# Scales of later weights found through DRAM, and spreads of keys and queries paced

## The chip, the cores and the metric

The kernel runs on one core of a Trainium2 chip. Its engines work side by side, each through its own queue of instructions in order: TensorE (PE; PEld is its loading of weights), VectorE (DVE), ScalarE (ACT), GpSimd (POOL) and SyncE (SP), whose queue issues nearly all transfers here. The metric is the device time of one execution in microseconds, and the median of several runs.

## The reference

Two attention layers of 32 heads with 20 features each read the same `x` (2048 rows of 640), and a gate per row mixes their outputs:

```python
def _A_ref(x, wqkv, wo):                      # _B_ref does the same with its own weights
    qkv = (x @ wqkv).reshape(B, S, 3, H, Dh).transpose(2, 0, 3, 1, 4)
    q, k, v = qkv[0], qkv[1], qkv[2]
    p = softmax(einsum("bhqd,bhkd->bhqk", q, k) * Dh ** -0.5, axis=-1)
    o = einsum("bhqk,bhkd->bhqd", p, v)
    return o.transpose(0, 2, 1, 3).reshape(B, S, D) @ wo

g = sigmoid((x * gate_w).sum(-1, keepdims=True))
return g * _A_ref(A_x, A_wqkv, A_wo) + (1 - g) * _B_ref(A_x, B_wqkv, B_wo)
```

All inputs and the output are float32.

## The kernel before, in words

**Numbers.** A product of float32 numbers is made from float16 parts: every operand is multiplied by a power of two, so that its largest number lies well in float16's range, and split into a high and a low part. So each kind of weight needs its largest absolute value over all 128 partitions. `largest` (L233) finds it in each partition on VectorE; a generator, `scales` (L167), carries it over the partitions: TensorE transposes the 128 maxima into one row (L173), VectorE takes the row's maximum (L177), four operations on bits make the power and its inverse (`powers`, L159), two products with the identity put them on a diagonal (L183), TensorE multiplies this by ones, which gives every partition both numbers (L190), and VectorE copies them out (L193) and hands them on (`set_qk`, `set_v`, or the function in `scales_o`). The first call, at the start, is for `x` and the first weights (five maxima). Twelve more stand among the work: three for queries and keys (two maxima each), seven for values and two for the output weights (one each).

**Staging.** Both layers together are 16 groups of four heads. A group takes 32 steps: four blocks of 512 queries, and for each eight steps over pairs of 128 keys. In a step TensorE makes eight products of scores (L639), ScalarE takes their exponentials (L642), and TensorE weighs the values of the step before (L657, in two blocks `V`). Beside this, 15 steps ahead, TensorE makes the scores again in the other direction (L581) and VectorE finds each query's maximum (L592, L589). The remaining room, one or two blocks of a step, goes to projections and output products (L382). Scores land in seven banks that rotate; who empties a bank (ScalarE or VectorE) frees it.

**What sets the order.** The program writes its own order: the strings `STEP` list a step's scores (`e`), maxima (`m`), blocks of values (`V`) and slots for one block of other work (`X`). Work with a date hangs in `todo` (`at(step, f)`); blocks wait in `fill` with a first step and a due step. Generators in `side` are moved on by `advance()`, once for each score, so eight times a step: such a move is called a turn, and a `yield` in a generator waits for the next. A generator that yields `PRODUCT` is parked until the next block of values, and its small product is put right ahead of that.

**Spreads.** A group's projected keys and queries lie in `cq` (two halves of 1024 tokens, `hl`), and `spread` (L433) copies them into the rows of `KT` and `QT` that the products want: 18 transfers a half, through `rows` (L424; issued in L428 and L430), all on SP's queue, one a turn. `spread_differences` (L474) adds four from `dd` to `KD`. The generator `later` (L490) starts them, a half at a time, ten turns after the half is projected and not before the group ahead has begun. When both halves are ready by then, both generators run side by side, and a turn has two transfers. `next_maxima` asks `spread_done` before a group's maxima are made.

**Other users of SP's queue** are the queries' maxima, which go through DRAM (`m_scr`: stored in L613, loaded in L617, five turns apart), the attention's outputs (L763), and the output products: `out_tiles` (L692) loads a tile of attention outputs (`o_in`, L699) and the sum so far (`y_out`, L704), waits `OWAIT` turns, and then puts its products in `fill`; their store is L732. SP executes its queue in order, a transfer that has to wait holds those behind it.

The body of the loop that calls all this:

```python
for what in (STEP[blocks] if maxima or some else LATE + " X" * (blocks == 2)).split():
    ...
    if what[0] == "e":
        ...
        advance()
    elif what == "V":
        product()
        if G:
            values(G - 1, k - 1)
```

Of the kernel before, what the change touches and what calls it, by code (L numbers as in the profile page):

```python
# [3 lines left out]

# [7 lines left out]
F32 = mybir.dt.float32  # L12
I32 = mybir.dt.int32
AF = mybir.ActivationFunctionType
OP = mybir.AluOpType
AX = mybir.AxisListType
# [3 lines left out]
P = 128  # L20
# [18 lines left out]
QUARTERS = (0, 128, 256, 384, 512)  # L39
FINE = (2, 3, 5, 6)  # L40
OB = 3
OWAIT = 20
AFROM, ADUE, ADUES = -24, -8, 4
QKMAX = (0, 10, 42, 10)
VEARLY = 338
# [23 lines left out]
def kernel(  # L69
# [48 lines left out]
    o_scr = [dram.tile([2, D, S], F16, name=f"o_scr{z}") for z in range(2)]  # L118
    m_scr = [dram.tile([4, 16, P], F16, name=f"m_scr{i}") for i in range(2)]
    y_scr = dram.tile([NT, P, D], F32, name="y_scr")  # L120


    clock = {"pe": 0.0, "done": 0.0, "act": 0.0, "dve": 0.0}
# [43 lines left out]
    def scales(maxima, n, then):  # L167

        for _ in range(REST):
            yield  # L170
        yield PRODUCT
        i, pt = take()
        nc.tensor.transpose(pt[:n, :P], maxima[:, :n], ident)  # L173
        tick_block(0.1, free_at[i])
        yield
        e = wts.tile([5, 8], F32, name="e", tag="scl", bufs=2)
        nc.vector.tensor_reduce(e[:n, 0:1], pt[:n, :P], axis=AX.X, op=OP.max)  # L177
        give(i, spend("dve", 0.3, clock["done"]))
        spend("dve", 1.0)
        powers(e.bitcast(I32)[:n, :], 1)  # L180
        dg = wts.tile([5, 2, 5], F32, name="dg", tag="scd", bufs=2)
        for k in range(2):
            nc.vector.tensor_scalar(dg[:n, k, :n], ident[:n, :n], e[:n, 3 + k:4 + k], None, op0=OP.mult)  # L183
        for _ in range(REST):
            yield
        yield PRODUCT
        i, pb = take()
        tick_block(0.1, free_at[i])
        for k in range(2):
            nc.tensor.matmul(pb[:, k * n:(k + 1) * n], ones[:n, :], dg[:n, k, :n], start=True, stop=True)  # L190
        yield
        both = wts.tile([P, 10], F32, name="both", tag="scb", bufs=2)
        nc.vector.tensor_copy(both[:, :2 * n], pb[:, :2 * n])  # L193
        give(i, spend("dve", 0.2, clock["done"]))
        then(both[:, :n], both[:, n:2 * n])

    def set_x(r_x, r, inv):
        nc.vector.tensor_copy(r_x, r)
        nc.vector.tensor_copy(inv_x, inv)

    def set_qk(i, r, inv):
        nc.vector.tensor_copy(r_qk[i], r)
        e = esc[i]
        nc.vector.tensor_tensor(e, inv[:, 0:1], inv_x, op=OP.mult)
        nc.vector.tensor_scalar(e, e, inv[:, 1:2], float(DH ** -0.5 / QKS ** 2), op0=OP.mult, op1=OP.mult)
        nc.vector.tensor_tensor(e, e, inv_x, op=OP.mult)

    def set_v(gg, r, inv):
        nc.vector.tensor_copy(r_v[gg], r)

        f = gg % (NG // 2) * 160
        while f < (gg % (NG // 2) + 1) * 160:
            p0 = f % P
            n = min(P - p0, (gg % (NG // 2) + 1) * 160 - f, (P, 32, 64, 32)[p0 // 32])
            nc.vector.tensor_copy(wrow[gg // (NG // 2)][p0:p0 + n, f // P:f // P + 1], inv[p0:p0 + n])
            f += n

    def scales_qk(i, maxima):

        return scales(maxima, 2, lambda r, inv: set_qk(i, r, inv))  # L220

    def scales_v(gg, maxima):
        return scales(maxima, 1, lambda r, inv: set_v(gg, r, inv))

    def scales_o(z, maxima):
        def then(r, inv):
            nc.vector.tensor_copy(r_o[z], r)
            nc.vector.tensor_scalar(f_o[z], gates[:, z, :], inv, inv_x, op0=OP.mult, op1=OP.mult)
            nc.vector.tensor_scalar(f_o[z], f_o[z], 1.0 / QKS, None, op0=OP.mult)

        return scales(maxima, 1, then)

    def largest(dst, src):  # L233
        nc.vector.tensor_reduce(dst, src, axis=AX.XY, op=OP.max,
# [198 lines left out]
    def spread(g, hl, t0, n, q=(0, 1), k=(0, 1), queues=repeat(nc.sync)):  # L433
# [5 lines left out]
        for j in range(2):  # L439
# [7 lines left out]
            if 1 in q:  # L447
# [2 lines left out]
                f = slice(r0 + 12 * j, r0 + 12 + 20 * j)  # L450
                yield from rows(qt[:, 1, cols], base, 8 * (1 - j), rk[g // 4][f, :, cols], 12 + 8 * j, False, queues)

    def project_r(i, ch):
        n = slice(ch * QB, (ch + 1) * QB)
        yield from project_chunk(blk["r", i], rk[i][:, 0, n], rk[i][:, 1, n], ch, QUARTERS if 4 * i in FINE else THIRDS)
        r_done.add((i, ch))
# [24 lines left out]
    def project_a(g, ch):  # L481
        if ch % 2 == 0:
            half_tiles(g)
        hl = blk["q", g]
        n = slice((ch % 2) * QB, (ch % 2 + 1) * QB)
        yield from project_chunk(blk["a", g], hl[:, 0, n], hl[:, 1, n], ch, QUARTERS if g in FINE else THIRDS)
        if ch == 1:
            key_differences(g, hl, work.tile([P, QB], F32, name="fs"), work.tile([P, 2, QB], F16, name="dd", bufs=1))
        if ch % 2 == 1:
            def later():  # L490
                for _ in range(10):
                    yield
                while not {(g // 4, c) for c in (ch - 1, ch)} <= r_done or now[0] < (g - 1) * NQ * NS + 1:
                    yield
                if ch == 1:
                    yield from spread_differences(g)
                yield from spread(g, hl, ch // 2 * 1024, 1024)
                spread_done.add((g, ch // 2))

            side.append(later())  # L500
# [478 lines left out]
    def at(G, f):  # L979
        todo.setdefault(G, []).append(f)  # L980
# [11 lines left out]
    for g in range(2 * NG):  # L992
        b = g * step
        n = g + 1
        if n < 2 * NG:
            parts = 4 if n in FINE else 3
            fill += [((-8, 15)[g] if g < 2 else b + AFROM, b + ADUE + ADUES * ch if g else 4 + 3 * ch, parts, project_a(n, ch))
                     for ch in range(4)]
            if n + 1 < 2 * NG:
                tasks(b + 2 if g else 9, 3, weights_a(n + 1))  # L1000
            i = g // 4 + 1
            if i < 4:
                if g % 4 == 0:
                    z, c0 = i // 2, 320 * (i % 2)
                    srcs = max_tasks([[(wqkv[z], part * D + c0 + 160 * k) for k in range(2)] for part in range(2)],
                                     lambda m, i=i: scales_qk(i, m))
                    tasks(b + QKMAX[i], 2, srcs)
                if g % 4 == 2:
                    tasks(b + 6, 3, weights_r(i))
                    parts = 4 if 4 * i in FINE else 3  # L1010
                    fill += [(b + 12, b + 22 + 4 * ch, parts, project_r(i, ch)) for ch in range(4)]
            gg = g // 2 + 1
            if gg < NG and g % 2 == 0:
                load, scale, split = weights_v(gg)
                at(max(b - 8, 0), load)
                if gg < NG - 1:
                    at(max(b - 5, 3), lambda scale=scale: side.append(scale()))
                at(max(b - 1, 7), split)
                fill += [(max(b + 2, 10), b + 2 * step - 4 + j // 2, 2, project_v(gg, j)) for j in range(0, NT, 2)]
    early = weights_v(NG - 1)  # L1020
    at(VEARLY, early[0])
# [164 lines left out]
```

## Time and profile before

| | |
|---|---|
| median of 3 runs | 2802.12 us (2801.08 to 2802.19) |
| the profiled execution | 2800.33 us, span 2798.5 us |
| mean granted TensorE clock | 0.995 |
| TensorE, VectorE, ScalarE, GpSimd busy | 98%, 88%, 90%, 24% |
| score products L639 | 4096, 1051.7 us |
| weighing of values L657 | 8192, 1082.2 us |
| issue of one spread on SP (kt<-cq, L428), median | 797 ns |
| DMA, mean busy share of 16 engines | 16.9% by the hardware queue q1 |

A row of waits reads "engine tile line <- who released it: us in total, times, longest us". A row of the timeline has the start in us from the span's start, the time in us, engine, line, operation, out<-in, forms, count, and in brackets the idle time just before and what ended it. A row of a group ends in "busy us, mean ns | idle us before <- releasers". A row of a stretch gives from:to, its length, then for PE, PEld, DVE, ACT and POOL the busy time and the number of instructions, the granted clock, the share of the DMA engines and GB/s. A row of one line's instructions has min/median/max in ns. A step runs here from the start of one first block of values to the next one.

### The profile page before, as it was taken

The numbers are of one execution on the slowest core, as the hardware profiler recorded it, in microseconds if no ns is written. First come the engines' busy times: TensorE is split into PE (matmuls) and PEld (weight loads), VectorE is DVE, ScalarE is ACT, GpSimd is POOL, SyncE is SP. The second block draws the span as 40 slices with busy tenths as digits, with TensorE's granted clock in tenths as the row PEclk, the third lists the DMA queues.
The fourth block names the chain that finished last, engine by engine and source line by source line (L and its number), as shares of the span: only waits on it lengthen the run. The fifth ranks groups of instructions, "written<-read, shape, count | busy, mean of one in ns | idle before, by whom it ended". The sixth has DMA issues, their size and how long they took to land.

```text
span 2798.5 us, 61863 instructions
## 1 busy us (share of the span) xinstructions
PE 2744.9 (98%) x23122; PEld 939.9 (34%) x23122; DVE 2452.3 (88%) x4795; ACT 2524.6 (90%) x5106; POOL 671.9 (24%) x914
## 2 busy tenths in 40 slices
PE   6999999999999999999999999999999999999998
PEld 3433332333333332333333323333333333322222
DVE  6789899889999999888888988989988898999982
ACT  3799999999999999999999889999999999989987
POOL 5322122312222421321221212222342202200111
PEclk9999999999999999999999999999999999999999
DMA  4020102001020211202012231122201112131112
GB/s 136 19 57 14 41 11 46 7 21 25 14 64 17 62 27 54 48 8 61 21 35 70 58 77 31 38 63 54 61 23 42 33 46 63 31 88 55 42 48 75
DMA packets 172943, 124.57 MB, mean 45 GB/s; under 512 B 103264, under 2 KB 142488, under 8 KB 172640
## 3 DMA queue, kind: packets, MB, share of 16 engines
q1 hardware_dynamic: 170096, 118.99, 16.9%
q8 instruction: 181, 2.97, 0.4%
q0 software_dynamic: 1600, 0.96, 0.2%
q14 instruction: 122, 1.00, 0.1%
q10 hardware_dynamic: 944, 0.66, 0.1%
HBM read 54.54 MB, written 31.85 MB: 31 GB/s over the span
## 4 chain that ended last, share of the span: by engine, by line
PE 92%; DVE 3%; ACT 2%; DMA 1%; POOL 1%; issue 1%; SPq 0%; POOLq 0%; ACTq 0%; DVEq 0%
PE acc L657 35%; PE bank L581 19%; PE bank L382 19%; PE bank L639 18%; DVE mpart L592 2%; ACT pt L642 1%; DMA xs<-in_A_x_dram 0%; ACT rl L585 0%; DMA wv<-in_A_wqkv_dram 0%; PE bank L820 0%; DVE rl L589 0%; PE bank L190 0%; SPq L428 0%; DVE ot L743 0%; PE bank L869 0%
## 5 line engine op out<-in xcount | busy, mean ns | idle before, releaser
L642 ACT ACTIVATE pt<-bank 128x512 f32<-128x512 f32 x4096 | 2169.2, 612 | 166.7 <-PE bank L639 101.7
L592 DVE TENSOR_REDUCE mpart<-bank 128x1 f32<-128x512 f32 x2976 | 1865.2, 682 | 222.2 <-PE bank L581 114.8
L657 PE MATMUL acc<-pt,v 128*21 128x512 f32 x8192 | 1082.2, 600 | 0.6 <-DVE ot L743 0.4
L639 PE MATMUL bank<-qt,kt 64*128 64x512 f16 x4096 | 1051.7, 380 | 4.2 <-ACT pt L642 2.0
L581 PE MATMUL bank<-kt,qt 60*128 60x512 f16 x3536 | 1021.3, 380 | 5.1 <-ACT pt L642 1.7
L581 PEld LDWEIGHTS <-qt 60*128 60x128 f16 x4096 | 238.1, 94 | 862.9 <-issue 802.9
L589 DVE CUSTOM_DVE_ANT_0 rl<-bank,rl 128x512 f32<-128x512 f32 x560 | 378.7, 680 | 16.7 <-ACT rl L585 10.6
L585 ACT ACTIVATE rl<-bank 128x512 f32<-128x512 f32 x560 | 329.7, 595 | 10.7 <-PE bank L581 8.7
L639 PEld LDWEIGHTS <-kt 64*128 64x128 f16 x4096 | 235.5, 94 | 238.7 <-issue 122.8
L382 PE MATMUL bank<-xx,wbh 128*128 128x168 f16 (+3 forms) x2400 | 286.0, 239 | 2.6 <-ACT xx L873 1.9
L657 PEld LDWEIGHTS acc<-pt,v 128*21 128x21 f32 x8192 | 143.1, 99 | 428.8 <-issue 421.9
L382 PE MATMUL bank<-xx,wbl 128*128 128x168 f16 (+3 forms) x1200 | 256.1, 237 | 0.0
L751 POOL TENSOR_TENSOR ot<-ot,sq 128x512 f32<-128x512 f32 x63 | 66.0, 1047 | 773.4 <-DVE sq L748 773.4
L382 PEld LDWEIGHTS <-wbh 128*128 128x128 f16 x2400 | 189.4, 98 | 109.5 <-issue 102.0
L581 PE MATMUL bank<-kd,qt 60*128 60x512 f16 x560 | 203.8, 380 | 1.6 <-DMA kd<-dd 1.2
L382 PE MATMUL bank<-woh,o_in 128*128 128x320 f16 (+1 forms) x640 | 156.4, 302 | 5.5 <-DMA o_in<-o_scr 5.4
L411 POOL CAST cq<-fs 128x512 f16<-128x512 f32 x60 | 36.6, 610 | 521.0 <-ACT fs L409 517.4
L382 PE MATMUL bank<-wvh,xx 128*128 128x160 f16 (+1 forms) x1280 | 155.2, 234 | 0.1
L382 PEld LDWEIGHTS <-xx 128*128 128x128 f16 x1920 | 131.5, 97 | 52.3 <-issue 49.1
L382 PE MATMUL bank<-wvl,xx 128*128 128x160 f16 (+1 forms) x640 | 137.3, 231 | 0.5 <-POOL wvl L322 0.5
L382 PEld LDWEIGHTS <-wbl 128*128 128x128 f16 x1200 | 117.4, 98 | 4.3 <-issue 0.8
L382 PEld LDWEIGHTS <-o_in 128*128 128x128 f16 (+1 forms) x960 | 80.9, 97 | 97.7 <-issue 63.8
(131 smaller groups left out, 1259.1 us busy)
## 6 DMA issues: line engine op xcount, KB each, us to landing
y_scr<-y_out SPq DMA_DIRECT2D x48, 320.0 KB
y_out<-y_scr SPq DMA_DIRECT2D x32, 320.0 KB
kt<-cq SPq DMA_DIRECT2D x120, 80.0 KB
o_scr<-on SPq DMA_DIRECT2D x240, 40.0 KB
o_in<-o_scr SPq DMA_DIRECT2D x64, 96.0 KB
kt<-cq SPq DMA_DIRECT2D x136, 40.0 KB
wstage<-in_B_wqkv_dram SPq DMA_DIRECT2D x13, 400.0 KB
xs<-in_A_x_dram SPq DMA_DIRECT2D x8, 640.0 KB
```

The lines of the kernel that those rows point to most:

```text
L382: nc.tensor.matmul(out_ap, a, b, start=(k == 0), stop=(k == len(pairs) - 1))
L411: nc.gpsimd.tensor_copy(hi, f)
L581: nc.tensor.matmul(pt, QT[g % 2][r, pair, q0:q0 + P], k, start=True, stop=True)
L585: nc.scalar.activation(relus[u, j], pt, AF.Relu)
L589: nc.vector.tensor_tensor_reduce(rl, pt, rl, 1.0, LOW, OP.add, OP.max, m)
L592: nc.vector.tensor_reduce(m, pt, axis=AX.X, op=OP.max)
L639: nc.tensor.matmul(et, KT[g % 2][r, pair, kt * P:(kt + 1) * P], QT[g % 2][r, pair, qb * QB:(qb + 1) * QB], start=True, stop=True)
L642: nc.scalar.activation(pt, et, AF.Exp, scale=factor(g // 4))
L657: nc.tensor.matmul(acc[32 * h:32 * h + VW, :], V[(g // 2) % 2][:, kt, (g % 2) * GH + h, :], ptiles.pop((G, kk, h)), start=(kt == 0), stop= ...
L751: nc.gpsimd.tensor_tensor(t3, t3, sq.unsqueeze(2).to_broadcast([P, 16, 32]), op=OP.mult)
```

## The change

Three things are changed.

The twelve later calls use a new generator, `scales_by_dram`. Two turns after the maxima are found, SP stores them in DRAM, each partition its one or two numbers in a row (`s_scr`, three buffers in turn). Ten turns later (`STORED`) SP loads the whole row, 128 or 256 numbers, into every partition (`srows`). 18 turns after that (`LOADED`) VectorE takes the maximum in every partition at once, `powers` works on all 128 partitions, and the results are handed on from there. TensorE has no part in it, and the diagonal and the copy are gone. Loading and scaling the values' weights are set one step earlier.

Spreads are paced: `paced(gen, n)` makes `n` turns of each yield of a spread, so that with `PACE` = 2 a transfer is issued in one of two turns, for all groups but group 1, which keeps one a turn. And the second half waits until the first is issued.

`OWAIT`, the turns between the issue of an output tile's loads and its products, is 24 instead of 20.

```diff
-OWAIT = 20
+STORED, LOADED = 10, 18
+OWAIT = 24
+PACE = 2
...
+    s_scr = [dram.tile([P * 2], F32, name=f"s_scr{i}") for i in range(3)]
+    scale_turns = counter()
...
+    def scales_by_dram(maxima, n, then):
+
+        turn = next(scale_turns)
+        flat = s_scr[turn % 3][:n * P]
+        yield
+        yield
+        nc.sync.dma_start(flat.rearrange("(p n) -> p n", n=n), maxima[:, :n])
+        for _ in range(STORED):
+            yield
+        rows = wts.tile([P, 2 * P], F32, name="srows", tag="srows", bufs=2)[:, :n * P]
+        nc.sync.dma_start(rows, flat.unsqueeze(0).to_broadcast([P, n * P]))
+        for _ in range(LOADED):
+            yield
+        e = wts.tile([P, 10], F32, name="es", tag="ses", bufs=2)
+        nc.vector.tensor_reduce(e[:, :n], rows.rearrange("p (q n) -> p n q", n=n), axis=AX.X, op=OP.max)
+        spend("dve", 0.35 * n + 0.5)
+        powers(e.bitcast(I32), n)
+        then(e[:, 3 * n:4 * n], e[:, 4 * n:5 * n])
...
     def scales_qk(i, maxima):
 
-        return scales(maxima, 2, lambda r, inv: set_qk(i, r, inv))
+        return scales_by_dram(maxima, 2, lambda r, inv: set_qk(i, r, inv))
...
-        return scales(maxima, 1, lambda r, inv: set_v(gg, r, inv))
+        return scales_by_dram(maxima, 1, lambda r, inv: set_v(gg, r, inv))
...
-        return scales(maxima, 1, then)
+        return scales_by_dram(maxima, 1, then)
...
+    def paced(gen, n):
+        for _ in gen:
+            for _ in range(n):
+                yield
...
+                while ch == 3 and (g, 0) not in spread_done:
+                    yield
+                turns_each = 1 if g == 1 else PACE
                 if ch == 1:
-                    yield from spread_differences(g)
-                yield from spread(g, hl, ch // 2 * 1024, 1024)
+                    yield from paced(spread_differences(g), turns_each)
+                yield from paced(spread(g, hl, ch // 2 * 1024, 1024), turns_each)
...
-                at(max(b - 8, 0), load)
+                at(max(b - 9, 0), load)
                 if gg < NG - 1:
-                    at(max(b - 5, 3), lambda scale=scale: side.append(scale()))
-                at(max(b - 1, 7), split)
+                    at(max(b - 6, 3), lambda scale=scale: side.append(scale()))
+                at(max(b - 1, 8), split)
```

Below is how it stands on three engines. The line numbers of the changed kernel are 31 higher in most of the program (L639 is L670, L657 is L688, L428 is L451, L699 is L730); `_94` and the like are buffer numbers.

On TensorE, ahead of a block of values of the last call (for the second layer's output weights), before:

```order
L581 MATMUL bank_93<-kt_83,qt_81 128x512
L639 LDWEIGHTS kt_83
L639 MATMUL bank_91<-qt_81,kt_83 128x512
L639 LDWEIGHTS kt_83
L639 MATMUL bank_92<-qt_81,kt_83 128x512
L190 MATMUL bank_89<-dg,ones 128x1 x2
L657 MATMUL acc<-pt,v_87 21x512 x4
```

and the same place now:

```order
L612 MATMUL bank_95<-kt_83,qt_81 128x512
L670 LDWEIGHTS kt_83
L670 MATMUL bank_91<-qt_81,kt_83 128x512
L670 LDWEIGHTS kt_83
L670 MATMUL bank_94<-qt_81,kt_83 128x512
L688 MATMUL acc<-pt,v_87 21x512 x4
```

The product with ones is gone, and the values follow the scores; the banks rotate differently. Apart from this TensorE's order is the same nearly everywhere: some blocks of other work change places with a step nearby.

On VectorE, the same call, first the half with the maximum and the diagonal as it was (the copy of the result stands eight rows further down):

```order
L592 TENSOR_REDUCE mpart<-bank_95 128x1
L177 TENSOR_REDUCE e<-bank_91 1x1
L162 TENSOR_SCALAR e<-e 1x1
L163 TENSOR_SCALAR e<-e 1x1
L164 TENSOR_SCALAR e<-e 1x1
L165 TENSOR_SCALAR e<-e 1x1
L183 TENSOR_SCALAR dg<-ident,e 1x1 x2
L592 TENSOR_REDUCE mpart<-bank_89 128x1
```

and now, all in one piece and some 30 rows later in the program:

```order
L623 TENSOR_REDUCE mpart<-bank_93 128x1
L215 TENSOR_REDUCE es<-srows 128x1
L166 TENSOR_SCALAR es<-es 128x1
L167 TENSOR_SCALAR es<-es 128x1
L168 TENSOR_SCALAR es<-es 128x1
L169 TENSOR_SCALAR es<-es 128x1
L250 COPY r_o_118<-es 128x1
L251 TENSOR_SCALAR f_o_120<-gates,es,inv_x 128x16
L252 TENSOR_SCALAR f_o_120<-f_o_120 128x16
L623 TENSOR_REDUCE mpart<-bank_95 128x1
```

The maximum reads the rows from DRAM instead of a bank, on 128 partitions instead of one, and the results follow it directly.

On SP's queue, where group 10 is spread (keys `kt_82`, queries `qt_80`; `o_in` and `y_out` are an output tile's loads), before:

```order
L430 DMA kt_82<-cq 20x1024
L430 DMA qt_80<-rk 20x1024
L613 DMA m_scr_124<-m4r 16x4x32 x4
L428 DMA qt_80<-cq 40x1x1024
L430 DMA qt_80<-cq 20x1024
L428 DMA qt_80<-rk 40x1x1024
L699 DMA o_in<-o_scr_121 128x2x128 x2
L704 DMA y_out<-y_scr 128x640
L430 DMA qt_80<-rk 20x1024
L617 DMA qt_81<-m_scr_124 4x512 x4
```

and now, between the two transfers of the maxima:

```order
L644 DMA m_scr_124<-m4r 16x4x32 x4
L453 DMA qt_80<-cq 20x1024
L451 DMA qt_80<-cq 16x1x1024
L730 DMA o_in<-o_scr_121 128x2x128 x2
L735 DMA y_out<-y_scr 128x640
L453 DMA qt_80<-cq 8x1024
L648 DMA qt_81<-m_scr_124 4x512 x4
```

Before, the maxima and the tile come near the end of the whole spread; now the spread's transfers stand further apart, and the maxima and the tile come in its first half.

More of the change, by code (lines that the diff above doesn't have):

```diff
@@ L2 @@
 from contextlib import ExitStack
-from itertools import cycle, repeat
+from itertools import count as counter, cycle, repeat
 import concourse.bass as bass
```

## The prediction

> **What bounds the kernel now.** I read the page's busy times and chain first, then the list of TensorE's waits, then the lines and places which the change touches.
>
> ```profile
> span 2798.5 us, 61863 instructions
> PE 2744.9 (98%) x23122; PEld 939.9 (34%) x23122; DVE 2452.3 (88%) x4795; ACT 2524.6 (90%) x5106; POOL 671.9 (24%) x914
> ...
> PE 92%; DVE 3%; ACT 2%; DMA 1%; POOL 1%; issue 1%; SPq 0%; POOLq 0%; ACTq 0%; DVEq 0%
> ```
>
> TensorE is busy for 98% of the span and carries 92% of the chain that ended last. What leaves its queue shortens the kernel; what leaves VectorE (88%) or the queues of transfers does so only where TensorE waits for it. Its waits:
>
> ```profile
> PE bank L869 <- DMA xs<-in_A_x_dram: 15.7, 2, 14.8
> PE bank L173 <- DVE wm L861: 6.4, 1, 6.4
> PE bank L382 <- DMA o_in<-o_scr: 5.4, 1, 5.4
> ```
>
> The first two are the start, which stays (the scales of x and of the first weights keep the old way). The third is one wait of 5.4 us for a late output tile.
>
> **Part 1: the scales leave TensorE.** Twelve calls change (three of queries and keys, seven of values, two of the output weights). Each had a transpose (L173) and a product with ones (L190; four matmuls in the trace, two operands in two passes), both put directly ahead of a block of values (L657).
>
> ```profile
> L173 PE MATMUL bank<-ident,m x12: 270/270/271, 128.1 to 1999.5; 128*1 128x128 f32 x9, 128*2 128x128 f32 x3
> ...
> L190 PE MATMUL bank<-dg,ones x52: 245/245/373, 29.3 to 2005.9; 1*128 1x1 f32 x36, 2*128 2x2 f32 x12, 5*128 5x5 f32 x4
> ```
>
> x12 are the transposes that go; of the 52 matmuls, 4 belong to the start and 48 go. How far each one held back the values behind it, in the last call:
>
> ```profile
> 1999.54 0.27 PE L173 MATMUL bank<-ident,m 128*1 128x128 f32 x1
> 1999.74 1.06 PE L657 MATMUL acc<-pt,v 128*21 128x512 f32 x8
> ...
> 2005.50 0.60 PE L190 MATMUL bank<-dg,ones 1*128 1x1 f32 x4 [0.35 <-ACT pt L642]
> 2006.03 1.06 PE L657 MATMUL acc<-pt,v 128*21 128x512 f32 x8
> ```
>
> From start to start that is 1999.74 - 1999.54 = 0.20 us and 2006.03 - 2005.50 = 0.53 us: the lower bound is 12 x 0.73 = 8.8 us. Ahead of the second stands another 0.35 us, because the product takes one of the seven banks and that one had still to be read by ScalarE. So I also price a call by whole steps. The stretches below are cut at the first value matmul of a step; each pair is two steps that hold a call, and the next two steps with the same blocks and no call.
>
> ```profile
> 424.26:434.99 10.73, 10.60 (x71) 2.56 (x70) 10.55 (x30) 9.11 (x19) 1.35 (x2) 1.00 0.09 21
> 434.99:444.25 9.26, 9.14 (x67) 2.15 (x65) 8.76 (x17) 8.94 (x19) 4.30 (x3) 1.00 0.05 11
> 871.27:882.82 11.55, 11.43 (x101) 3.91 (x99) 10.85 (x29) 10.40 (x22) 3.23 (x4) 1.00 0.34 88
> 882.82:892.77 9.95, 9.95 (x96) 3.50 (x95) 8.68 (x17) 9.12 (x20) 0.25 (x1) 1.00 0.00 0
> ...
> 1997.76:2009.52 11.76, 11.41 (x101) 4.47 (x99) 11.09 (x30) 9.97 (x21) 1.05 (x1) 1.00 0.23 68
> 2009.52:2019.97 10.45, 10.45 (x100) 3.82 (x101) 9.20 (x19) 9.88 (x21) 2.62 (x6) 1.00 0.03 3
> 439.65:444.25 4.60, 4.57 (x35) 1.08 (x33) 4.38 (x9) 4.52 (x10) 0.00 (x0) 1.00 0.10 22
> 444.25:449.09 4.84, 4.63 (x34) 1.07 (x32) 4.72 (x10) 4.76 (x11) 0.00 (x0) 1.00 0.25 58
> ```
>
> The differences are 1.47, 1.60 and 1.31 us, 1.46 in the mean: 12 x 1.46 = 17.5 us, the upper bound. I take it rather than 8.8, since it is measured where the work is and includes the waits for a bank.
>
> Some comes back. VectorE's rows:
>
> ```profile
> L599 DVE TENSOR_REDUCE mneg<-mpart 128x16 f32<-128x64 f32 x64 | 14.0, 218 | 5.1
> L183 DVE TENSOR_SCALAR dg<-ident,e 1x1 f32<-1x1 f32 (+2 forms) x26 | 4.3, 201 | 0.1
> L177 DVE TENSOR_REDUCE e<-bank 1x1 f32<-1x128 f32 (+2 forms) x13 | 3.5, 270 | 0.5 <-PE bank L173 0.5
> L193 DVE COPY both<-bank 128x2 f32<-128x2 f32 (+2 forms) x13 | 1.9, 149 | 1.0 <-PE bank L190 1.0
> L162 DVE TENSOR_SCALAR e<-e 1x1 int32<-1x1 int32 (+2 forms) x13 | 1.8, 141 | 0.4
> ```
>
> A call loses 0.27 + 2 x 0.20 + 0.15 = 0.82 us there and gains a maximum over 128 or 256 numbers of each partition: 0.22 us by L599's 64 numbers, 0.27 by L177's 128, so about 0.3. The four steps of 0.14 us that make powers stay. VectorE gets 12 x 0.5 = 6 us less, hidden behind TensorE. But it now has maximum, powers and copies in one piece of 0.3 + 0.56 + 0.5 = 1.4 us, where before they were two, and a late VectorE gives banks back late. The last two stretches above price such a piece: the second has a transpose and a reciprocal of 0.97 us more on VectorE and is 0.24 us longer; steps with three more blocks of TensorE take it at almost nothing. Between 0 and 0.24 I take 0.12: 12 x 0.12 = 1.4 us. Part 1 is 17.5 - 1.4 = 16.1 us.
>
> The new way issues 24 transfers more on SP's queue, 4 to 8 turns of a step ahead of anything due. A step has eight turns (one per score), so the load is issued ten turns (about 6 us) after the store, and VectorE reads it 18 turns later: 18/8 x 4.6 us = 10 us at least.
>
> ```profile
> DMA to landing us min/median/max: 1.6/2.0/2.5
> ...
> SPq L617 <- DMA m_scr<-m4r: 47.2, 54, 2.8
> ```
>
> The first row is the landing of the small transfers of kd, at most 2.5 us. The second is a way through DRAM that is there already: its load is issued five turns (3 us) after its store and SP stands 47.2/54 = 0.9 us for it, 2.8 at worst. So a store lands in 4 to 6 us, inside the new ten turns, and the load has four times what it needs. I cost these waits at nothing; VectorE's ten us are the cover. The values' load and scale go one step earlier, so their split has its numbers as before; nobody else moves for it.
>
> **Part 2: paced spreads.** Why was the tile late at 1656?
>
> ```profile
> 1617.25 0.85 SPq L428 DMA_DIRECT2D kd<-dd  x1
> ...
> 1648.74 0.73 SPq L430 DMA_DIRECT2D qt<-rk  x1
> ...
> 1654.24 0.92 SPq L699 DMA_DIRECT2D o_in<-o_scr  x2
> ...
> 1656.32 0.45 PE L382 MATMUL bank<-woh,o_in 128*128 128x320 f16 x1 [5.39 <-DMA o_in<-o_scr]
> ...
> L428 SPq DMA_DIRECT2D kt<-cq x136: 762/797/1121, 40.5 to 2491.1; - x136
> ...
> 1642.60:1647.58 4.98, 4.98 (x40) 1.49 (x38) 4.78 (x10) 4.58 (x10) 3.17 (x5) 1.00 0.45 127
> 1647.58:1659.42 11.84, 6.45 (x40) 1.61 (x38) 5.13 (x10) 5.04 (x11) 0.00 (x0) 0.75 0.37 90
> ```
>
> SP needs 0.80 us to issue one spread. With both halves of a group spreading at once, two per turn, a step asks 16 x 0.8 = 12.8 us of a queue that has 5. From 1617 to 1656 it issues without a gap, and o_in's loads stand behind spreads that are not urgent. The step that waits takes 11.84 us against 4.98 for its neighbour of the same blocks, in which the granted clock was 1.00 against 0.75: 6.9 us, of which 5.4 are the wait and 1.5 the slower matmuls after it. With one transfer in two turns, one half after the other, spreads take 4 x 0.8 = 3.2 us of a step and SP keeps up, so o_in issues where the program has it, 24 turns (14 us) ahead of its product. I take the whole 6.9 us; the bounds are 0 (the wait returns elsewhere) and 6.9.
>
> What becomes late is the spread: counted in the program, that of group 10 ends in step 298 and not 291, and its first reader is step 306: 8 steps, 40 us, for 2.5 us of landing. The buffer it reads is written again from step 299 (first half, free since 294) and 312. So nothing is priced there. The longer wait of output tiles (24 turns, not 20) lets products of the next fill the slot; the number of blocks per step hardly changes, so 0.
>
> **Sum.** 16.1 + 6.9 = 23.0 us from the profiled execution's 2800.33 us (span 2798.5): 2777.3. The median of the runs is 1.8 us above it, so 2779 us, 0.8% less.
>
> **Rivals.**
> *Only the bare matmuls come back* (17%). The waits around them were VectorE's and ScalarE's lag, which the one piece of 1.4 us keeps alive. For it: VectorE is at 10.55 of 10.73 us in the first pair. Against it: the second pair has 0.7 us of slack and still shows 1.60. 2802.1 - 8.8 - 6.9 = 2786 us.
> *The wait for o_in stays or moves to another tile* (12%): SP still has stores of outputs among the spreads, and waits there for VectorE. 2802.1 - 16.1 = 2786 us.
> *The products weren't the cost* (4%): VectorE's work set those steps and it stays; only part 2 counts: 2795 us.
> *VectorE waits for the broadcast rows* (4%), the slower side. Its store writes pieces of 4 or 8 bytes; store and load together have 28 turns, 28/8 x 5 = 17.5 us at some 5 us a step, against some 8 by the rows above. VectorE executes in order, so each us beyond that holds all maxima behind it, their banks, and TensorE. It decides once a call is late by 23.0/12 = 1.9 us, at 19.4 us from store to read. At 25 us the cost is 12 x 7.5 = 90 us: 2779 + 90 = 2869 us. Against it: no transfer in these rows needs half of that.
> The Trainium skill's page "DMA: Bandwidth & Descriptors" (Specifications) speaks for this rival: pieces below 512 B make the engine read, modify and write. The way of m_scr, in pieces of 64 bytes, shows no such delay beyond its 4 to 6 us; pieces of 4 bytes no run here shows.
>
> **How the numbers follow.** The forecast (both parts as summed) has 62%, with a range of its own from 2772 (some waits for a bank of other steps go too) to 2784. The two cases at 2786 have 29%, the others 8%, 1% is unnamed. The range for 8 in 10 runs from 2772 to 2793: its upper end leaves out the late broadcast and the case of part 2 alone, and allows the two at 2786 half of each other's loss. About 0.2% (5.6 us) can be told from no change. Forecast, both cases at 2786 and most of the case at 2795 are faster: 93%; same 3%; slower 4%.
>
> **What would show it.** Right: L173 and L190 only at the start, with 4 matmuls; TensorE's list without o_in; steps of the former calls within 0.3 us of their neighbours; SP's spreads with gaps between them; VectorE's new maximum without idle time ahead of it. Wrong: idle time of VectorE ended by the rows from DRAM, a wait of TensorE for kt, qt or o_in, or steps with calls that are still 1 us longer.

## The result and the profile after

The changed kernel takes 2784.53 us (median of 4 runs, 2783.47 to 2784.95) against 2802.05 us before (2801.08 to 2802.19): a ratio of 0.9937, 95% interval [0.9925, 0.9949]. That is 17.5 us less, and 5.5 us above the 2779 us that were forecast. The profiled execution took 2784.79 us, at a mean granted clock of 0.996.

The head of its page, with the chain of work that ended last:

```profile
span 2782.9 us, 61802 instructions
PE 2731.9 (98%) x23062; PEld 933.6 (34%) x23062; DVE 2447.3 (88%) x4759; ACT 2522.9 (91%) x5106; POOL 673.0 (24%) x914
...
PE 91%; DVE 5%; ACT 1%; DMA 1%; POOL 1%; issue 1%; SPq 0%; POOLq 0%; DVEq 0%; ACTq 0%
```

TensorE has the 60 matmuls less that were to go (23122 to 23062). Its share of the chain fell by a point and VectorE's rose from 3% to 5%. TensorE's waits in the changed kernel:

```profile
PE bank L900 <- DMA xs<-in_A_x_dram: 15.4, 2, 14.5
PE bank L177 <- DVE wm L892: 6.8, 1, 6.8
PE bank L670 <- DVE mpart L623: 3.9, 15, 0.7
...
PE bank L612 <- DVE mpart L623: 1.2, 6, 0.2
```

The wait for `o_in` is gone. In its place stands a row for banks that VectorE's maxima had not yet read. In the kernel before, the same rows were these:

```profile
PE bank L639 <- DVE mpart L592: 1.5, 7, 0.2
...
PE bank L581 <- DVE mpart L592: 0.8, 4, 0.2
```

The stretches of the changed kernel that answer to the prediction's are cut in the same way. In each of the first three pairs, the first stretch has lost its transpose and product, and the second has received VectorE's new piece. The last pair is the place where the step of 11.84 us was.

```profile
422.99:432.19 9.20, 9.15 (x66) 2.13 (x65) 8.62 (x17) 9.02 (x19) 0.97 (x1) 1.00 0.12 29
432.19:442.01 9.82, 9.22 (x66) 2.25 (x64) 9.65 (x25) 9.21 (x19) 4.80 (x3) 1.00 0.37 80
868.07:878.02 9.95, 9.95 (x97) 3.50 (x95) 9.27 (x18) 9.63 (x21) 3.23 (x4) 1.00 0.03 5
878.02:888.32 10.30, 10.30 (x97) 3.40 (x95) 9.57 (x25) 9.89 (x22) 0.60 (x1) 1.00 0.39 101
1981.91:1992.55 10.64, 10.64 (x97) 3.89 (x95) 9.81 (x19) 10.08 (x21) 1.05 (x1) 1.00 0.30 63
1992.55:2004.02 11.47, 10.77 (x96) 3.79 (x95) 10.38 (x27) 9.88 (x21) 2.63 (x6) 1.00 0.35 84
1635.68:1640.63 4.95, 4.95 (x40) 1.48 (x38) 4.74 (x10) 4.55 (x10) 0.00 (x0) 1.00 0.34 76
1640.63:1645.59 4.96, 4.96 (x41) 1.51 (x39) 4.76 (x10) 4.63 (x10) 0.00 (x0) 1.00 0.43 128
```

Against the six stretches of before, the first stretches are shorter by 10.73 - 9.20 = 1.53, by 1.60 and by 1.12 us, 1.42 in the mean: the gain at these places was there, in the size that was forecast. But the second ones are longer by 9.82 - 9.26 = 0.56, by 0.35 and by 1.02 us, 0.64 in the mean, where the prediction allowed 0.12. The last pair is even: the step that waited is as short as its neighbour, at a granted clock of 1.00.

The sum over all steps, from the first to the last, is 2658.3 us against 2675.2: 16.9 less. (The first step itself began 1.2 us later in this execution; over several executions of these kernels that varied by 1 us either way.) Put down to their places these are 7.3 us from the two steps around the former wait, 17.5 from the steps that lost a product, -7.3 from those that received the piece, and -1.2 from steps that exchanged blocks of output products: 16.3, so 0.6 us stays with no place of its own. (Near 1090 us steps of two kinds overlap. In the run of the scales alone, below, where no blocks moved, the same steps lose 18.3 us and get 7.6 back.)

How a piece costs time can be seen in the last call. VectorE in the changed kernel (start, duration):

```profile
1997.47 0.69 DVE L623 TENSOR_REDUCE mpart<-bank 128x1 f32<-128x512 f32 x1
1998.08 0.28 DVE L215 TENSOR_REDUCE es<-srows 128x1 f32<-128x128 f32 x1
...
1999.03 0.40 DVE L251 TENSOR_SCALAR f_o<-gates,es,inv_x 128x16 f32<-128x16 f32 x1
1999.45 0.23 DVE L252 TENSOR_SCALAR f_o<-f_o 128x16 f32<-128x16 f32 x1
1999.54 0.68 DVE L623 TENSOR_REDUCE mpart<-bank 128x1 f32<-128x512 f32 x1
```

and TensorE beside it:

```profile
1999.21 0.37 PE L670 MATMUL bank<-qt,kt 64*128 64x512 f16 x1
2000.28 0.37 PE L670 MATMUL bank<-qt,kt 64*128 64x512 f16 x1 [0.70 <-DVE mpart L623]
```

The piece runs from 1998.08 to 1999.54. The maximum behind it begins 1.5 us later than it would have without the piece, so its bank comes free as much later; the banks rotate, the next score needs just this one, and TensorE stands 0.70 us.

### The profile page after: what moved, and what is told of

The parts are those of the page before. It is cut to its first block, busy times and chain, and to the rows that moved or that the text cites. A ratio compares the mean times of both kernels' runs of the same rounds, so it can differ in the third digit from the quotient of the medians.

```text
span 2782.9 us, 61802 instructions
## 1 busy us (share of the span) xinstructions
PE 2731.9 (98%) x23062; PEld 933.6 (34%) x23062; DVE 2447.3 (88%) x4759; ACT 2522.9 (91%) x5106; POOL 673.0 (24%) x914
## 4 chain that ended last, share of the span: by engine, by line
PE 91%; DVE 5%; ACT 1%; DMA 1%; POOL 1%; issue 1%; SPq 0%; POOLq 0%; DVEq 0%; ACTq 0%
PE acc L688 35%; PE bank L405 19%; PE bank L612 19%; PE bank L670 18%; DVE mpart L623 3%; ACT pt L673 1%; DVE rl L620 1%; DMA xs<-in_A_x_dram 0%; ACT rl L616 0%; PE bank L851 0%; DMA wv<-in_A_wqkv_dram 0%; DVE ot L774 0%; PE bank L900 0%; DMA wstage<-in_A_wqkv_dram 0%; DMA m_scr<-m4r 0%
## 5 line engine op out<-in xcount | busy, mean ns | idle before, releaser
L688 PE MATMUL acc<-pt,v 128*21 128x512 f32 x8192 | 1081.7, 600 | 1.7 <-DVE ot L774 1.6
L670 PE MATMUL bank<-qt,kt 64*128 64x512 f16 x4096 | 1052.0, 380 | 7.6 <-DVE mpart L623 3.9
L670 PEld LDWEIGHTS <-kt 64*128 64x128 f16 x4096 | 235.6, 94 | 240.1 <-issue 123.2
L688 PEld LDWEIGHTS acc<-pt,v 128*21 128x21 f32 x8192 | 143.0, 99 | 436.8 <-issue 429.4
L405 PEld LDWEIGHTS <-xx 128*128 128x128 f16 x1920 | 131.5, 97 | 52.2 <-issue 49.1
```

Source lines behind the costliest of these rows:

```text
L405: nc.tensor.matmul(out_ap, a, b, start=(k == 0), stop=(k == len(pairs) - 1))
L670: nc.tensor.matmul(et, KT[g % 2][r, pair, kt * P:(kt + 1) * P], QT[g % 2][r, pair, qb * QB:(qb + 1) * QB], start=True, stop=True)
L688: nc.tensor.matmul(acc[32 * h:32 * h + VW, :], V[(g // 2) % 2][:, kt, (g % 2) * GH + h, :], ptiles.pop((G, kk, h)), start=(kt == 0), stop= ...
```

## The experiments

The first question was whether the two parts and the longer `OWAIT` add up to the whole. The next was what sets the price of the piece: VectorE's time in one lump, or the banks that the program chose because `spend` told it too little of VectorE's time. The last was how much of the time allowed for the way through DRAM it needs.

### The three parts apart

The scales alone are the changed kernel with

```diff
-OWAIT = 24
-PACE = 2
+OWAIT = 20
+PACE = 1
...
-                while ch == 3 and (g, 0) not in spread_done:
-                    yield
```

> The changed kernel with spreads as before (one transfer a turn, halves side by side) and the tiles' wait of 20 turns: only the scales go through DRAM. If the two parts add up, it keeps what the steps with calls lost, 16.9 - 7.3 = 9.6 us by the two traces from the first step to the last, and the wait for o_in near 1650 us stays: some 2792 us. The rival, that the wait goes because the transfers are moved by the new scales too, gives some 2785 us, with no wait for o_in in TensorE's list.

Measured: 2791.54 us, 0.996 [0.9946, 0.9973]. Its waits of TensorE have both rows, the old and the new:

```profile
PE bank L405 <- DMA o_in<-o_scr: 6.0, 1, 6.0
PE bank L668 <- DVE mpart L621: 4.1, 16, 0.7
```

Over its steps it is 9.8 us shorter than before. The wait for `o_in` was 0.7 us longer in this execution than before, so the scales are worth about 10.5 us, not 16.1: 0.88 us a call, where the bare matmuls are 0.73 and the forecast had 1.34.

The pacing alone is the kernel before with

```diff
+PACE = 2
...
+                while ch == 3 and (g, 0) not in spread_done:
+                    yield
+                turns_each = 1 if g == 1 else PACE
...
-                yield from spread(g, hl, ch // 2 * 1024, 1024)
+                yield from paced(spread(g, hl, ch // 2 * 1024, 1024), turns_each)
```

(and the same for `spread_differences`).

> The kernel before with paced spreads alone (scales on TensorE, 20 turns). Adding up gives 2802.1 - 7.3 = 2794.8 us, and no wait for o_in. The rival, that it takes the 24 turns as well, gives 2796 to 2802 us, with a shorter wait for o_in left.

Measured: 2793.91 us, 0.9969 [0.9957, 0.9981]. The steps are 7.3 us shorter in sum, 6.9 of it in the step that waited and 0.4 in the one behind it; nothing else moved. Part 2 was sized right.

Of the pacing, the wait of one half for the other was then kept and the gaps left out:

```diff
-PACE = 2
+PACE = 1
```

> The kernel before with the second half of a spread waiting for the first, but one transfer a turn: it tells which half of the pacing counts. A step then asks 8 x 0.8 = 6.4 us of SP's queue in some 5.3 us, so SP falls behind by 1 to 2 us a step for five steps; o_in has 20 turns (13 us) of lead. Theory: that is enough, no wait of TensorE for o_in, 2794 to 2795 us as with the full pacing. Rival: SP's queue has to have gaps; then part of the wait is left, 2796 to 2802 us.

Measured: 2793.85 us, 0.9972 [0.9961, 0.9983], the same gain, with no wait for `o_in` in TensorE's list:

```profile
1640.83 0.92 SPq L708 DMA_DIRECT2D o_in<-o_scr  x2
```

The tile's first product comes at 1651.9, so its load is issued 11 us ahead, where before it was 2.1 (1654.24 and 1656.32). So one half after the other is enough, and a free turn between transfers is not needed. SP's queue has no need of gaps either, as the changed kernel shows at the same place:

```profile
1618.33 0.82 SPq L451 DMA_DIRECT2D kt<-cq  x1
...
1625.10 0.91 SPq L730 DMA_DIRECT2D o_in<-o_scr  x2
...
1646.63 0.75 SPq L453 DMA_DIRECT2D qt<-rk  x1
1650.53 0.34 SPq L763 DMA_DIRECT2D y_scr<-y_out  x1
```

From 1618 to 1647 SP issues almost without a pause, as before. But `o_in` is issued at 1625.10, 18.8 us ahead of its product (1643.9).

The longer `OWAIT` alone is one number in the kernel before:

```diff
-OWAIT = 20
+OWAIT = 24
```

> The kernel before with 24 turns instead of 20 alone. If SP's queue is the cause, the products only come four turns (2.6 us) later to the same late tile: the wait falls from 5.4 to about 2.8 us, part of the slow clock after it stays or goes, some 2798 to 2800 us. The rival, that 24 turns were what helped, gives 2795 us and no wait.

Measured: 2803.19 us, 1.0002 [0.9993, 1.0011]. The wait is still there, 5.44 us instead of 5.39:

```profile
1655.46 0.92 SPq L699 DMA_DIRECT2D o_in<-o_scr  x2
...
1657.45 0.45 PE L382 MATMUL bank<-woh,o_in 128*128 128x320 f16 x1 [5.44 <-DMA o_in<-o_scr]
```

The wait did not fall to 2.8 us as expected, because the product did not move: TensorE comes to it 3.3 us after the start of the same step as before. The four turns changed the places of other products, but not of this one, so this run doesn't tell whether more time for this tile would have helped. Over the steps it is 1.2 us longer than before, in the places where blocks of output products moved to other steps (183 to 192, 305 and 306, 447 to 460, 487 to 496). One row of TensorE's waits grew by as much; before, and with 24 turns, it is

```profile
PE acc L657 <- DVE ot L743: 0.4, 2, 0.2
...
PE acc L657 <- DVE ot L743: 1.6, 5, 0.9
```

The three new waits, of 0.87, 0.18 and 0.20 us, stand at the first values of steps 184, 448 and 488, each the start of a block of queries: VectorE has not yet read the sums of the block ahead out of `acc`. All traces with 24 turns have 1.2 to 1.6 us in this row, all with 20 have 0.4. The reverse, the changed kernel with `OWAIT` at 20:

> The changed kernel with 20 turns instead of 24 for output tiles. The kernel before lost 1.2 us by the 24 turns in the two traces (first to last step), in places where blocks of output products changed steps (183 to 192, 447 to 460, 487 to 496). If that and not the start is it, this takes 1 us less than the changed kernel, some 2783.4 us, and the same places no longer differ from the kernel before. The rival, that with both parts in 24 turns are needed, shows a wait of TensorE for o_in and a longer time.

Measured: 2782.74 us, 0.9934 [0.992, 0.9947]; its steps are 1.3 us shorter than the changed kernel's, in the same places. Both runs point the same way, but in the times the difference (1.8 us, with ranges that overlap) is not resolved.

The three parts together: in the traces -9.8 - 7.3 + 1.2 = -15.9 us (-16.6 with the longer wait of the first taken out), against -16.9 of the whole; in the medians, against 2802.4 us of the same batch, -10.9 - 8.5 + 0.8 = -18.6 against -17.5. They add up, and the shortfall lies in the scales.

### What the piece on VectorE costs

If the choice of banks were at fault, telling the program the piece's true length should help, since the program takes the bank that it expects to be free first, by what `spend` was told:

```diff
-        spend("dve", 0.35 * n + 0.5)
+        spend("dve", 0.3 * n + 1.3)
```

> The changed kernel in which the program's own account of VectorE is told 0.3 n + 1.3 us for a call instead of 0.35 n + 0.5. Instructions and their order stay, only the banks rotate differently. Rival to the theory of the one piece: a wrong account chose banks that were not free; then the loss of 0.4 to 1.1 us a call goes, to some 2780 us. Theory: there are seven banks and a late VectorE holds three or more of them, any choice waits; 2784 to 2785 us, not more than 2 us less than the changed kernel.

Measured: 2784.76 us, 0.9941 [0.9927, 0.9954]; the steps' sum is 2658.7 against 2658.3 us. The order of instructions stayed as it was on every engine; only the banks rotate differently, and with them the waits:

```profile
PE bank L670 <- ACT pt L673: 3.4, 12, 0.5
PE bank L612 <- ACT pt L673: 3.0, 10, 0.5
PE bank L670 <- DVE mpart L623: 2.2, 10, 0.2
```

Waits of TensorE went from VectorE's banks to ScalarE's (in the changed kernel these rows have 2.0, 1.7 and 3.9 us), and the time stayed the same. So a wrong account of VectorE's time is not the cause, and the engine named in such a row depends on which bank happens to be next.

If the time on VectorE is what costs, a longer piece must cost more. This repeats the maximum three times over, about 0.86 us more for a call of one number:

```diff
+        for _ in range(3):
+            nc.vector.tensor_reduce(e[:, :n], rows.rearrange("p (q n) -> p n q", n=n), axis=AX.X, op=OP.max)
```

> The changed kernel with the new maximum over the rows made four times instead of once (three times more than is needed), so VectorE's piece is 0.83 us longer in nine calls and 1.2 us in three. Theory: the piece has used up what the banks hide, so nearly all of the 9 x 0.83 + 3 x 1.2 = 11 us comes on top: 2793 to 2796 us. Rival, the price of the prediction (0.12 us for a piece of 1 us): 2785 to 2787 us.

Measured: 2800.45 us, 0.9995 [0.9986, 1.0004]: 15.9 us lost, nearly the whole gain of the change, for some 12 us more of VectorE. Its waits of TensorE, and the three stretches that hold a piece (above 9.82, 10.30 and 11.47 us):

```profile
PE bank L672 <- DVE mpart L625: 10.1, 25, 2.5
PE bank L614 <- DVE mpart L622: 4.1, 5, 1.4
```

```profile
435.59:446.39 10.80, 9.65 (x67) 2.32 (x65) 10.53 (x28) 9.48 (x19) 4.79 (x3) 1.00 0.34 73
883.36:894.62 11.26, 10.49 (x97) 3.49 (x95) 10.42 (x28) 10.49 (x23) 1.48 (x2) 1.00 0.35 95
2007.37:2019.79 12.42, 10.78 (x95) 3.79 (x95) 11.22 (x30) 9.46 (x20) 2.62 (x6) 1.00 0.31 76
```

0.98, 0.96 and 0.95 us more, for pieces that are 0.97, 0.96 and 0.95 us longer from their first start to the next maximum's: once the piece is longer than what the banks can cover, each further microsecond costs one at these places. The 11 us that were expected are too few: the twelve pieces are 12.7 us longer together, and the steps 16.8. The largest excess is at 273 us, where a piece longer by 1.5 us costs 3.1.

If it is the lump that costs, cutting it should give some back. Here the maximum, the powers in two halves and the results stand two turns apart, with the first of them six turns earlier:

```diff
-STORED, LOADED = 10, 18
+STORED, LOADED = 10, 12
...
-        spend("dve", 0.35 * n + 0.5)
-        powers(e.bitcast(I32), n)
+        spend("dve", 0.35 * n)
+        yield
+        yield
+        for k in range(2):
+            powers(e.bitcast(I32), n, k)
+            spend("dve", 0.25)
+            yield
+            yield
```

> The changed kernel with the new work of VectorE cut in four (maximum; two powers; two powers; the copies and factors), two turns apart, and the wait for the rows shortened by six turns, so that it ends at the same turn. Theory: what came back (0.42 to 1.06 us in the step of each call) came from one piece of 1.4 us that gave banks back late; cut, it costs under 0.2 us a call, so 5 us less than the changed kernel: 2779 to 2780 us, and TensorE's waits for VectorE's maxima ahead of scores fall from 3.9 us to about 1.5. Rival: VectorE's time as such counts, and the time stays at 2784 to 2785 us.

Measured: 2779.99 us, 0.9919 [0.9906, 0.9933]: 4.5 us below the changed kernel, and 3.2 us in the steps' sum. The expected sign in the list of waits did not come: TensorE's wait for VectorE's maxima ahead of scores fell from 3.9 to 3.1 us only, not to 1.5, and the one for ScalarE there rose from 2.0 to 3.0, so the gain is read from the steps. Where it came from is uneven. Two stretches of the changed kernel that hold a piece (two steps, and one):

```profile
1599.07:1609.92 10.85, 10.67 (x79) 2.78 (x77) 10.68 (x28) 9.28 (x19) 1.49 (x2) 1.00 0.00 1
1766.03:1771.66 5.63, 5.43 (x41) 1.31 (x39) 5.48 (x17) 5.30 (x12) 2.34 (x2) 1.00 0.00 0
```

and the same two with the piece cut, followed by two others, the first of them with the two steps ahead of it:

```profile
1597.81:1607.71 9.90, 9.90 (x78) 2.98 (x77) 9.75 (x23) 9.17 (x19) 1.49 (x2) 1.00 0.00 1
1763.81:1768.76 4.95, 4.95 (x41) 1.41 (x39) 4.91 (x13) 4.62 (x10) 2.54 (x2) 1.00 0.00 0
...
422.13:431.92 9.79, 9.54 (x66) 2.11 (x65) 8.57 (x18) 9.64 (x20) 0.97 (x1) 1.00 0.11 27
431.92:441.88 9.96, 9.38 (x65) 2.15 (x64) 9.59 (x26) 8.54 (x18) 4.80 (x3) 1.00 0.35 79
1989.23:2000.72 11.49, 10.58 (x96) 3.81 (x95) 10.91 (x27) 9.92 (x21) 2.62 (x6) 1.00 0.35 84
```

The first two gain 0.95 and 0.68 us, since parts of the piece now stand in neighbouring steps in which VectorE has time. The other two gain nothing: 9.96 against 9.82 (VectorE is busy for 9.59 of it, so cutting the piece makes no room), and 11.49 against 11.47. The two steps ahead of the 9.96, in which the piece now begins, are longer too, 9.79 against 9.20. There the wait for the rows, six turns shorter, was too short:

```profile
430.46 0.28 DVE L218 TENSOR_REDUCE es<-srows 128x1 f32<-128x128 f32 x1 [0.78 <-DMA srows<-s_scr]
```

VectorE stood so at three of the twelve calls, 1.6 us in all, and the steps of these waits are 1.2 us longer. That belongs to the shorter wait, not to the cut. In the last stretch a single operation is long. On VectorE, and then on GpSimd:

```profile
1994.85 1.26 DVE L260 TENSOR_SCALAR f_o<-gates,es,inv_x 128x16 f32<-128x16 f32 x1
```

```profile
1994.86 1.16 POOL L444 TENSOR_TENSOR cq<-fs,cq 128x512 f16<-128x512 f32 x1
```

The operation took 1.26 us where the same one took 0.40 (1999.03 above), and TensorE stood 0.91 us for the bank of a maximum behind it. The cut also moved the first parts of the piece up to six turns ahead. No run moved the whole piece without cutting it, so how much of the gain is the cut and how much the move stays open. The last experiment on the piece has both, the cut and `OWAIT` at 20:

> The piece cut in four, and 20 turns for output tiles: if the two add up, 2780.0 - 1.2 = 2778.8 us, the fastest of all. If they do not, 2780 us or more.

Measured: 2780.09 us, 0.9925 [0.9912, 0.9939], the same as the cut alone. In the traces it has 0.8 us less over the steps, but 0.7 of it in two of the steps in which VectorE stands for the rows (0.8 us in all here, not 1.6); in the times no difference can be seen. At 2780 us these two are the fastest of all versions tried.

### How long the way through DRAM takes

The waits in turns are cut from 10 and 18 to 2 and 4, so that the transfers' own time shows:

```diff
-STORED, LOADED = 10, 18
+STORED, LOADED = 2, 4
```

> The changed kernel with 2 turns between the store and the load of the rows instead of 10, and 4 turns from the load to VectorE's maximum instead of 18: it measures how long the way through DRAM really takes. 4 turns are about 2.6 us, with the wait for the store inside. If a store and a load land in about 2 us each, the load leaves some 0.7 us late and VectorE stands some 0 to 2 us ahead of each maximum: 12 x 1 = 12 us at most, 2785 to 2797 us, with VectorE's idle time ended by the rows. The rival mechanism of the prediction (pieces of 4 bytes land late) gives waits of 5 us and more for each call, 2840 us or more.

Measured: 2871.5 us, 1.0253 [1.0239, 1.0267], the rival's case. The waits of VectorE, of SP and of TensorE:

```profile
DVE es L215 <- DMA srows<-s_scr: 62.3, 12, 8.2
```

```profile
SPq L211 <- DMA s_scr<-m: 70.7, 12, 8.0
```

```profile
PE bank L612 <- DVE mpart L623: 35.6, 9, 7.3
PE bank L670 <- DVE mpart L623: 29.5, 16, 8.0
```

From the end of the store's issue to the issue of the load that waits for it are 7.0 to 8.1 us in the nine calls whose piece is 4 bytes, and 2.8 to 3.2 us in the three whose piece is 8 bytes (queries and keys). From the load to VectorE's reading are 4.0 to 5.3 us. Against the changed kernel's 2784.5 us this is 87 us more: TensorE stands 65.1 us in its two rows, and the mean granted clock is 0.981 instead of 0.996. So a call of one number needs 12 to 13 us from store to reading. In the changed kernel's trace 16.5 to 25.9 us pass, but not always where they are needed: SP was late with one load, which left it 5.8 us (427.89 to 433.69), against the 4.2 to 5.3 that such a load took here. To see whether the size of the piece does it, the calls of one number were given two equal columns, so that all twelve store pieces of 8 bytes:

```diff
+        k = n
+        if n == 1:
+            pair = wts.tile([P, 2], F32, name="pair", tag="pair", bufs=2)
+            for j in range(2):
+                nc.vector.tensor_copy(pair[:, j:j + 1], maxima[:, :1])
+            maxima, n = pair, 2
...
-        then(e[:, 3 * n:4 * n], e[:, 4 * n:5 * n])
+        then(e[:, 3 * n:3 * n + k], e[:, 4 * n:4 * n + k])
```

with the waits at 2 and 4 turns as in the experiment above.

> The kernel with the short waits (2 and 4 turns, 2871.5 us), in which the nine calls with one number a partition store it twice, so that each piece is 8 bytes and not 4, as it is in the three calls of queries and keys. There a store of 4-byte pieces took 7.4 to 8.4 us from its issue to the load behind it, one of 8-byte pieces 3.1 to 3.6 us. If the size of the piece decides, all twelve take 3.1 to 3.6 us, VectorE's wait ahead of the maximum falls from 62 us in all to some 20 to 25 us, and the time by about as much: some 2825 to 2835 us. Rival: the calls for values and output weights are late for where they stand, and the time stays at 2865 us or more.

Measured: 2819.73 us, 1.0064 [1.0047, 1.0081], 52 us less than with pieces of 4 bytes:

```profile
DVE es L221 <- DMA srows<-s_scr: 23.1, 11, 3.2
```

All twelve stores now land in 2.4 to 3.1 us. So the size decides, of the piece or of the whole row, which grew with it from 512 to 1024 bytes. Why twice the bytes land in less than half the time is not settled by these runs. The traces narrow it down: in their records of DMA packets the 128 pieces of a store start 0.8 to 1.3 us after its issue and take some 9 ns each, with 4 bytes as with 8, so the difference lies between these packets and the moment at which SP learns that they have landed.

## Why the prediction was right, and where its sum was off

**The number.** The 2784.5 us are 5.5 above the forecast of 2779, half a microsecond above the range that the prediction gave to its own case (2772 to 2784), and inside the one for 8 in 10. The first rival's 2786 us is nearer.

**What bounds it.** Right on the whole: both parts gained by taking time, or a wait, from TensorE's queue. At the places of the pieces it was VectorE that set the time: its longer piece added 15.9 us with not one matmul more.

**Part 1, the 17.5 us of the products.** Right in size, and the choice between the bounds too: the steps that lost a product are shorter by 1.46 us in the mean, 1.42 in the three pairs shown. With the bare matmuls (8.8 us) and the 7.3 that came back, the scales alone would have gained 1.5 us, not 10. How much of the 1.46 is the products, and how much VectorE's own work, which left the same steps, no run here separates. The first rival is wrong in that the waits around the products did go from their steps. But its reason, that one piece keeps VectorE's lag alive, is what happened in the step where the piece now stands, and the 10.5 us that the scales are worth lie nearer to its 8.8 than to the forecast's 16.1.

**Part 1, the 1.4 us that return.** This is the term that failed: 12 x 0.12 us predicted, 12 x 0.61 = 7.3 measured. It was bounded by one pair of steps (4.60 and 4.84 us) in which 0.97 us more on VectorE were taken to cost 0.24, so the piece of 1.4 to 1.5 us was priced by a shorter piece, and then at half of that. The two rows were read too kindly: VectorE is busy for 4.72 us against 4.38, only 0.34 more, since the reciprocal begins at 449.07, at the end of the stretch. So 0.24 us was most of what was added, not a quarter. The longer piece shows that the price is no constant share: beyond the cover, 0.95 us cost 0.95. The prediction's saving of 6 us of VectorE's time was true as an average (2452.3 to 2447.3) and beside the point, since TensorE waits for one bank at one place. "Steps of the former calls within 0.3 us of their neighbours" failed for the same reason: the neighbours now hold the piece.

**Part 2.** Right: 6.9 predicted, 7.3 in the changed kernel and with the pacing alone. Its account of SP's queue was partly wrong. The spreads have no gaps from 1618 to 1647, and the gaps were not what helped; what counted is that the tile's loads stand early enough in the queue. The rival that the wait stays or moves falls: TensorE's list holds no late tile of outputs, keys or queries, but for one wait of 1.2 us for `kd` at the start (at 58 us), which was there before.

**`OWAIT` at nothing.** About 1.2 us lost in the traces, in both directions of the test, not resolved in the times. It stands as waits for `acc`, in the places where blocks moved. The wait for `o_in` was not touched by it, since the product kept its place.

**The way through DRAM at nothing.** Right for the changed kernel: VectorE's maximum has no idle time ahead of it. But the ten us "at least" from load to reading were 5.8 at one place, and the 4 to 6 us for a store were an estimate from stores of 64-byte pieces, and stores of 4 bytes take 7 to 8. In the changed kernel SP had to wait for them after all:

```profile
SPq L211 <- DMA s_scr<-m: 17.8, 3, 7.4
SPq L648 <- DMA m_scr<-m4r: 89.6, 54, 7.2
```

So the rival of a late broadcast has a true mechanism, and only the turns allowed keep it away. With 6 turns in place of 28 it gave 2871.5 us, and with 22, in the run with the piece cut, VectorE already stood 1.6 us for the rows. The Trainium skill's page "DMA: Bandwidth & Descriptors" (Specifications) says that pieces below 512 B are read, modified and written. That holds for 4 bytes and for 8 alike, so it doesn't by itself give the difference that these runs show.

**The sum.** 17.5 - 7.3 + 7.3 - 1.2 = 16.3 us in place of 23.0: 5.9 of the 6.7 us that are missing are the piece on VectorE, 1.2 are `OWAIT`, and the stall gave 0.4 more. The rival in which the products weren't the cost falls with the 10.5 us of the scales alone.

## What to carry to other kernels

Work that is taken from the engine that bounds and put on its neighbour in one lump is priced by the buffers that rotate between the two, not by the neighbour's mean load: here a lump longer than the slack of the rotation cost its excess in full, at the place where it stood. So cut it into parts between the maxima and put them in steps where the neighbour has time; in the steps where it has none, cutting gave nothing. When a transfer is late, look at when it was issued before changing how long its reader waits: here a longer wait did not even move the product in question, and putting one burst after the other, so that the load was issued 11 us ahead and not 2, removed the stall.

## What the hardware showed that was not expected

A store of 128 pieces of 4 bytes to DRAM was slower than one of 128 pieces of 8 bytes: 7.0 to 8.1 us from the end of its issue to the next transfer that waits for it, against 2.4 to 3.2.

Other stores were late with it. SP's wait for `m_scr` was 47.2 us in all and 2.8 at worst before, 52.2 and 2.9 with the pacing alone, but 89.6 and 7.2 in the changed kernel and 76.5 and 7.1 with the scales alone. The changed kernel's trace shows which ones: six times such stores are issued within 3 us behind one of 4-byte pieces, and these are the six waits over 3.2 us (6.2 to 7.2); they end 8.5 to 9.4 us after the slow store's issue. Behind a store of 8-byte pieces alone none is over 2.7. With the short waits, where SP first waits for the slow store itself, the longest is 3.2 with pieces of 4 bytes and 2.9 with 8. That these stores queue behind the slow one fits, but no run tests it; TensorE didn't wait for it.

The operation of 1.26 us on VectorE began with a two-input operation of GpSimd and ended with it (1994.85 to 1996.11, and 1994.86 to 1996.02). With the cut and `OWAIT` at 20 it took 1.20 us at the same place. The Trainium skill's page "SBUF — State Buffer" (Who interferes with whom) says that a VectorE instruction in a mode with two ports competes with GpSimd for a shared port pair: whichever engine issues first has the pair for its whole instruction, and the other one blocks. This trace agrees, with 1.26 us where 0.28 to 0.40 was enough; which mode the operation ran in it doesn't show. Not every operation waits: in the changed kernel four of 0.14 to 0.15 us, on one number a partition (from 1998.39 on), ran unhindered beside such an operation of GpSimd (1998.18 to 1999.34). No run here moved GpSimd's operation away.
